# Softcap attention followed by a bilinear feed-forward: a list schedule fixes the order of all five queues

## The chip, the cores and the metric

The kernel runs on one core of one Trainium2 chip. The metric is device time in microseconds (us) of one execution; each version is run several times and the median is compared.

## The reference

```
scale = 1.0 / np.sqrt(q.shape[-1])                     # q, k, v: (4, 12, 448, 64) float32
scores = scale * np.matmul(q, k.transpose(0, 1, 3, 2))
scores = cap * np.tanh(scores / cap)                   # cap = 30
scores = scores - np.max(scores, axis=-1, keepdims=True)
attn = np.exp(scores)
attn = attn / (np.sum(attn, axis=-1, keepdims=True) + 1e-09)
attn_out = np.matmul(attn, v)
x = attn_out.transpose(0, 2, 1, 3).reshape(1792, 768)
out = (x @ w_a) * (x @ w_b) @ w_out                    # w_a, w_b: (768, 1536); w_out: (1536, 768), float64
```

## The kernel before

Attention works on 24 **pairs** (two heads of one batch side by side on the 128 partitions); the feed-forward (FFN) on two **groups** of 896 tokens, and a group needs the output of 12 pairs. This gives three stages: the attention of pairs 0 to 11; the attention of pairs 12 to 23 with the FFN of group 0 put between; the FFN of group 1 alone.

A pair goes through these steps. `load_pair` fetches k and q in eight pieces and v in one, on SP's queue. `prep_pair` turns k and q on DVE (line 213); from pair 12 on each is also split into a rounded high part and the rest (lines 217, 218), and products are made of three parts. `scores` does four chunks of keys, three of 128 for each head and a last one that takes 64 of either: PE writes the chunk into PSUM (line 239, from pair 12 on lines 244 and 247), ACT makes the tanh (line 248) and, for two chunks at once, the exp (line 249), and DVE adds the chunks up for the denominators (lines 253, 256, 257). `attend` multiplies by v (line 269; the last chunk on line 271, a matmul on 64 rows for each head). `normalize` sums over the partitions with matmuls against a selecting matrix (line 282, eight of 112 columns), takes the reciprocal on DVE (line 290), stores it to DRAM as `rd` (line 291) and reads it back spread over 64 partitions for each head as `den` (line 295). `scale` multiplies (line 301), and `split_x` makes the two parts that the FFN reads (lines 310, 311); for the second group they go through DRAM as `xd` and `xl`.

In the FFN a slice of 128 hidden units makes four `ph` products of 18 matmuls with 448 columns (lines 403 to 405), which ACT and DVE empty (lines 408 to 412); after three slices come 14 `po` products of nine matmuls with 384 columns (lines 434 to 436, emptied on lines 438 and 440). Weights come as 64-bit floats: `load64` fetches a tile, `ready_w` converts it in six steps (two on ACT, lines 361 and 362, three on DVE, one on POOL, line 366) and stores it as `wd` for the second group, `split_w` splits it (lines 385, 386).

PSUM holds two score buffers of two banks (`ps_sc`) and four single banks (`ps_1`) for everything else. The order of each queue is the framework's: the loop at the end of the function calls the steps in the order of a string, `run_ffn` advances the FFN generator, and the framework's scheduler then places the instructions by its own estimates, save those marked `keep_in_program_order`.

Of the kernel before, what the change touches and what calls it, by code (L numbers as in the profile page):

```python
# [9 lines left out]
F32 = mybir.dt.float32  # L10
# [107 lines left out]
def kernel(  # L118
# [16 lines left out]
    CP = 112  # L135
    NCH = S // CP
# [13 lines left out]
    PFB = 2  # L150
    Q = 32
    AHEAD = 4
    STRETCH = 1.25

# [4 lines left out]
    rd = [dr.tile([2 * NCH, CP], F32, tag=f"rd{i}", name=f"rd{i}") for i in range(NPAIR)]  # L159
    xd = [dr.tile([P, S], F32, tag=f"xd{i}", name=f"xd{i}") for i in range(NPG)]  # L160
    top = ctx.enter_context(tc.tile_pool(name="top", bufs=1))
    ident = top.tile([P, P], F32, tag="ident", name="ident")
# [7 lines left out]
    pp = fast.enter_context(tc.tile_pool(name="pp", bufs=PFB))  # L170
# [3 lines left out]
    ps_sc = fast.enter_context(tc.tile_pool(name="ps_sc", bufs=2, space=bass.MemoryType.PSUM))  # L174
    ps_1 = fast.enter_context(tc.tile_pool(name="ps_1", bufs=4, space=bass.MemoryType.PSUM))
# [4 lines left out]
    sel = const.tile([P, 2, Q], F32, tag="sel", name="sel")  # L180
# [4 lines left out]

    kz = [const.tile([P, P], F32R, tag=f"kz{x}", name=f"kz{x}") for x in "hl"]


# [4 lines left out]
    def load_pair(pi):  # L193
        b, hp = divmod(pi, NP)
        for nm, src in (("k", k), ("q", q)):
            t = ld.tile([P, S // BLK, BLK], F32, tag=f"ld{nm}", name=f"ld{nm}_{pi}")
            for j in range(2):
                for h in range(D // BLK):
                    rows = slice(j * D + h * BLK, j * D + (h + 1) * BLK)
                    cols = src[b, 2 * hp + j, :, h * BLK : (h + 1) * BLK]  # L200
                    eng = nc.scalar if nm == "q" and pi == 0 else nc.sync
                    eng.dma_start(t[rows], cols.rearrange("(c p) d -> p c d", p=BLK))
            raw[nm, pi] = t
        t = ld.tile([P, 2 * NC3 + 1, D], F32, tag="ldv", name=f"ldv_{pi}", bufs=3)
        nc.sync.dma_start(t, v[b, 2 * hp : 2 * hp + 2].rearrange("j s d -> (j s) d").rearrange("(c p) d -> p c d", p=P))
        raw["v", pi] = t

    def prep_pair(pi):
        stk[pi] = []
        for nm in "kq":  # L210
            t = raw.pop((nm, pi))
            tt = qk.tile([P, S], F32, tag=f"t{nm}", name=f"t{nm}_{pi}")
            nc.vector.transpose(tt, t.rearrange("p c d -> p (c d)"))
            if pi >= NPG:
                hi = qk.tile([P, S], F32R, tag=f"h{nm}", name=f"h{nm}_{pi}", bufs=1)
                lo = qk.tile([P, S], F32R, tag=f"t{nm}", name=f"l{nm}_{pi}")
                nc.scalar.copy(hi, tt)
                nc.vector.tensor_sub(lo, tt, f32(hi))
                tt = (hi, lo)
            stk[pi].append(tt)  # L220
        if pi >= NPG:
            for z, x in zip(kz, stk[pi][0]):
                for j, o in enumerate(own):
                    nc.gpsimd.tensor_copy(z[o, j * R : (j + 1) * R], x[o, krem[j] : krem[j] + R])
# [3 lines left out]
    def scores(pi, hf):  # L228
        tk, tq = stk[pi]
        pf = pp.tile([P, 4 - hf, S], F32, tag=f"pf{hf}", name=f"pf_{pi}_{hf}")  # L230
        for i in range(2):
            c = 2 * hf + i
            n = 2 if c < NC3 else 1
            psc = ps_sc.tile([P, 2, 512], F32, tag="pssc", name=f"psc_{pi}_{c}")
            if pi < NPG:
                for j, o in enumerate(own):
                    at = j * R + c * P if n == 2 else krem[j]
                    to = psc[:, j, :S] if n == 2 else psc[o, 0, :S]
                    nc.tensor.matmul(to, tk[o, at : at + (P if n == 2 else R)], tq[o], start=True, stop=True)  # L239
# [312 lines left out]
```

## Time and profile before

| | |
|---|---|
| median of 3 runs | 762.07 us (759.05 to 763.45) |
| profiled execution | 757.11 us, of which the span from the first to the last instruction 755.2 |
| mean granted clock of TensorE (PE) in it | 0.987 of full speed |
| PE busy | 715.5 us, 95% of the span |
| DVE, ACT, POOL busy | 450.7, 337.4, 141.0 us |

The profile is of one execution. "Busy" is time in which an engine worked on an instruction; a wait is put down to the semaphore that came last. A row of the timeline gives the start, the time, the instruction, and in brackets the idle time before it and what ended it; matmuls overlap, so the time that one costs is read from one start to the next. A float32 matmul shows as two rows.

### The profile page before, as it was taken

What the parts mean: (1) busy time and instruction counts of PE and PEld (TensorE: products, weight loads), DVE (VectorE), ACT (ScalarE), POOL (GpSimd) and SP (SyncE); (2) the same over time, 40 slices, a digit from 0 to 9 for tenths busy, and PEclk for the clock granted to TensorE, in tenths of its full rate; (3) what the DMA queues carried; (4) which work ended last, traced back from release to release, by engine and by line L of the source; (5) the groups of instructions that cost most, each with busy time, mean ns of one, the idle gap of its engine ahead of it and who ended that gap; (6) DMA issues with size and microseconds to landing.
All of it is one profiled execution on the core that took longest, in us unless ns stands there. A gap on an engine that the chain in (4) does not pass through costs nothing.

```text
span 755.2 us, 10285 instructions
## 1 busy us (share of the span) xinstructions
PE 715.5 (95%) x3948; PEld 571.1 (76%) x3948; DVE 450.7 (60%) x648; ACT 337.4 (45%) x426; POOL 141.0 (19%) x160
## 2 busy tenths in 40 slices
PE   5978978999999998999989999999999999999996
PEld 1322225687778777778768789999999999999996
DVE  4687999877856687686785755733124334344322
ACT  5776888665675574375544531021322102102200
POOL 0000135335505444065340310000000000000000
PEclk9999998999999999999999999999999999999999
DMA  7585697675746666254540334632022102201012
GB/s 131 111 170 113 143 226 181 149 232 186 209 107 184 198 180 171 54 159 163 180 162 25 116 119 138 202 104 80 27 62 63 63 22 73 74 22 43 1 42 109
DMA packets 136951, 90.49 MB, mean 120 GB/s; under 512 B 114624, under 2 KB 122560, under 8 KB 136896
## 3 DMA queue, kind: packets, MB, share of 16 engines
q1 hardware_dynamic: 125856, 48.64, 26.4%
q0 software_dynamic: 9184, 40.90, 16.5%
q8 instruction: 33, 0.54, 0.3%
q10 hardware_dynamic: 1856, 0.23, 0.2%
q14 instruction: 22, 0.18, 0.1%
HBM read 67.24 MB, written 22.50 MB: 119 GB/s over the span
## 4 chain that ended last, share of the span: by engine, by line
PE 55%; DMA 17%; DVE 12%; ACT 6%; issue 5%; SPq 2%; POOL 2%; ACTq 0%; DVEq 0%; POOLq 0%
PE po L434 6%; PE po L436 6%; PE po L435 6%; PE pha L405 5%; PE pha L404 5%; PE pha L403 5%; PE phb L405 5%; PE phb L404 5%; PE phb L403 5%; DMA rd<-rec 4%; DMA w64a<-in_moe_w_a_dram 3%; DMA den<-rd 3%; DMA w64o<-in_moe_w_out_dram 3%; PE pv L269 2%; DMA ldk<-in_k_dram 2%
## 5 line engine op out<-in xcount | busy, mean ns | idle before, releaser
L434 PE MATMUL po<-who,gh 128*128 128x384 f32 x336 | 114.5, 341 | 3.5 <-DVE acc L440 2.0
L435 PE MATMUL po<-wlo,gh 128*128 128x384 f32 x336 | 113.7, 338 | 0.0
L436 PE MATMUL po<-who,gl 128*128 128x384 f32 x336 | 113.3, 338 | 0.4 <-DVE gl L412 0.4
L403 PE MATMUL pha<-xhi,wha 128*128 128x448 f32 x288 | 106.1, 368 | 0.0
L404 PE MATMUL pha<-xlo,wha 128*128 128x448 f32 x288 | 105.6, 367 | 0.0
L405 PE MATMUL pha<-xhi,wla 128*128 128x448 f32 x288 | 105.2, 365 | 0.0
L404 PE MATMUL phb<-xlo,whb 128*128 128x448 f32 x288 | 104.9, 364 | 0.0
L403 PE MATMUL phb<-xhi,whb 128*128 128x448 f32 x288 | 104.8, 364 | 0.0
L405 PE MATMUL phb<-xhi,wlb 128*128 128x448 f32 x288 | 104.5, 363 | 0.0
L248 ACT ACTIVATE pf<-psc,capt 128x896 f32<-128x896 f32 x96 | 84.1, 909 | 26.8 <-PE psc L244 12.2
L249 ACT ACTIVATE pf<-pf,capt 128x1792 f32<-128x1792 f32 (+1 forms) x48 | 77.1, 1606 | 1.0
L440 DVE TENSOR_TENSOR acc<-po,acc 128x384 f32<-128x384 f32 x84 | 45.7, 551 | 41.4 <-PE po L436 41.0
L434 PEld LDWEIGHTS po<-who,gh 128*128 128x128 f32 x336 | 63.6, 189 | 7.3 <-DVE acc L440 3.0
L269 PE MATMUL pv<-pf,ldv 128*64 128x448 f32 x288 | 63.3, 554 | 1.6 <-ACT pf L249 1.2
L435 PEld LDWEIGHTS po<-wlo,gh 128*128 128x128 f32 x336 | 63.6, 189 | 1.6 <-issue 1.4
L436 PEld LDWEIGHTS po<-who,gl 128*128 128x128 f32 x336 | 63.5, 189 | 1.6 <-DVE gl L412 1.0
L239 PE MATMUL psc<-tq,tk 64*128 64x448 f32 (+1 forms) x192 | 50.0, 629 | 15.0 <-ACT pf L248 8.0
L410 DVE TENSOR_TENSOR asb<-phb,asb 128x448 f32<-128x448 f32 x48 | 29.7, 619 | 56.8 <-PE phb L405 56.8
L411 ACT CAST gh<-asb 128x448 fp32r<-128x448 f32 x48 | 27.1, 564 | 75.5 <-DVE asb L410 75.2
L403 PEld LDWEIGHTS pha<-xhi,wha 128*128 128x128 f32 x288 | 54.5, 189 | 6.9 <-issue 2.4
L404 PEld LDWEIGHTS pha<-xlo,wha 128*128 128x128 f32 x288 | 54.5, 189 | 5.2 <-issue 1.1
L403 PEld LDWEIGHTS phb<-xhi,whb 128*128 128x128 f32 x288 | 54.0, 188 | 5.2 <-issue 1.3
(99 smaller groups left out, 1040.8 us busy)
## 6 DMA issues: line engine op xcount, KB each, us to landing
w64o<-in_moe_w_out_dram POOLq DMA_DIRECT2D x12, 768.0 KB, 5.8
w64a<-in_moe_w_a_dram POOLq DMA_DIRECT2D x11, 768.0 KB, 6.3
w64b<-in_moe_w_b_dram POOLq DMA_DIRECT2D x11, 768.0 KB, 6.4
ldk<-in_k_dram SPq DMA_DIRECT2D x96, 56.0 KB
ldv<-in_v_dram SPq DMA_DIRECT2D x24, 224.0 KB
den<-rd SPq DMA_DIRECT2D x48, 112.0 KB
ldq<-in_q_dram SPq DMA_DIRECT2D x92, 56.0 KB
out_dram<-acc SPq DMA_DIRECT2D x13, 384.0 KB
```

Source lines behind the costliest of these rows:

```text
L239: nc.tensor.matmul(to, tk[o, at : at + (P if n == 2 else R)], tq[o], start=True, stop=True)
L248: nc.scalar.activation(pf[:, 2 * i : 2 * i + n], psc[:, :n, :S], AF.Tanh, scale=capt[:, 1:2])
L249: nc.scalar.activation(pf, pf, AF.Exp, scale=capt[:, 0:1])
L269: nc.tensor.matmul(t[j * D : (j + 1) * D, :S], tv[:, j * (NC3 + 1) + c], p, start=(c == 0), stop=False)
L403: nc.tensor.matmul(t[:, :S], wh[:, kk], xhi[:, kk, cs], start=(kk == 0), stop=False)
L404: nc.tensor.matmul(t[:, :S], wh[:, kk], xlo[:, kk, cs], start=False, stop=False)
L405: nc.tensor.matmul(t[:, :S], wl[:, kk], xhi[:, kk, cs], start=False, stop=(kk == NK - 1))
L410: nc.vector.tensor_mul(asb[h], t[:, :S], asb[h])
L434: nc.tensor.matmul(t[:, :HALF], gh[:, cs], wh, start=(f == fs[0]), stop=False)
L435: nc.tensor.matmul(t[:, :HALF], gh[:, cs], wl, start=False, stop=False)
L436: nc.tensor.matmul(t[:, :HALF], gl[:, cs], wh, start=False, stop=(f == fs[-1]))
L440: nc.vector.tensor_add(acc[:, ti, hs], t[:, :HALF], acc[:, ti, hs])
```

## The change

All steps become small functions, and each call of one is a job with an engine, a time, a lag and a list of jobs that it needs. The order of PE's jobs is written out (`chain`); every job gets a latest time from the jobs after it, and a list scheduler in the kernel (the last loop below) plays the five engines forward and takes on each the ready job that is due first. The instructions are then issued in that order inside `manual_schedule`, in which the framework moves nothing.

With it come these changes. All four chunks of a pair's scores stand together in the first stage, and two and two in the second. `attend` uses a matmul on 128 rows for the last chunk too, against a copy of v that is zero in the other head's rows. The sums have 14 matmuls of 64 columns in place of eight of 112, and are written into the free columns of the bank of `pv`. PSUM has three score buffers and two `pv` banks in the first stage; in the second two score buffers, one `pv` bank and three FFN banks (the first six FFN products have two). v is loaded in four pieces, for pairs 2 to 11 on POOL's queue; weights after the sixth are fetched, and all `wd` stored, on SP's queue and not POOL's. Weight tiles are taken in the order in which slices need them. The copies for the last chunk (`last_keys`) move from POOL to ACT. Three matmuls on zeros (`warm`) stand ahead of the first scores, and the identity matrix is no longer made on the usual path.

```diff
-    ps_sc = fast.enter_context(tc.tile_pool(name="ps_sc", bufs=2, space=bass.MemoryType.PSUM))
-    ps_1 = fast.enter_context(tc.tile_pool(name="ps_1", bufs=4, space=bass.MemoryType.PSUM))
+    room = {"pv": psum_pool("pv_one", 2), "sc": psum_pool("sc_one", 3)}
...
+        eng = nc.gpsimd if 2 <= pi < NPG else nc.sync
+        if n < 2:
+            part = slice(n * (NC3 + 1), n * (NC3 + 1) + NC3)
+            eng.dma_start(t[:, part.start + n : part.stop + n], src[:, part])
+        else:
+            eng.dma_start(t[own[n - 2], NC3 + n - 2], src[own[n - 2], NC3])
...
-        for c in range(NC3):
-            for j in range(2):
-                p = prob[pi, c // 2][:, 2 * (c % 2) + j]
-                nc.tensor.matmul(t[j * D : (j + 1) * D, :S], tv[:, j * (NC3 + 1) + c], p, start=(c == 0), stop=False)
-        for o in own:
-            nc.tensor.matmul(t[o, :S], tv[o, NC3], prob[pi, 1][o, 2], start=False, stop=True)
...
+        for c in range(2 * hf, 2 * hf + 2):
             for j, o in enumerate(own):
+                p = prob[pi, hf][:, 2 * (c % 2) + (j if c < NC3 else 0)]
+                nc.tensor.matmul(t[o, :S], tv[:, j * (NC3 + 1) + (c if j == 0 else (c + 1) % (NC3 + 1))], p, start=(c == 0), stop=(c == NC3))
...
+                to = t[i * Q : (i + 1) * Q, S : S + SC]
+                nc.tensor.matmul(to, sel[:, m], psum[pi % 2][:, j, c * SC : (c + 1) * SC], start=(m == 0), stop=last)
...
+        if n == 0:
+            room["sc"] = psum_pool("sc_two", 2, "sc_one")
+            room["ff", 0] = psum_pool("ff_a", 2)
+        elif n == FB0:
+            room["pv"] = psum_pool("pv_two", 1, "pv_one")
+            room["ff", 1] = psum_pool("ff_b", 1)
...
+    for pi in range(NPG):
+        for c in range(SUB):
+            scores_of(pi, c)
+        if pi:
+            attend_of(pi - 1)
...
+    ffn(3.6)
+    for pi in range(NPG, NPAIR + 1):
+        attend_of(pi - 1)
+        if pi < NPAIR:
+            for c in range(2):
+                scores_of(pi, c)
+            ffn(GAP / 2)
+            for c in range(2, SUB):
+                scores_of(pi, c)
+            ffn(GAP / 2)
...
+        t, e, xs_ = best
+        x = min((x for x in xs_ if max(x.ready, port if x.shared else 0.0) <= t), key=lambda x: x.due - (SOON if x.fn in (gate, keep_a, collect) else 0.0))
+        (line if e == "PE" else wait[e]).remove(x)
+        x.start, x.end = t, t + x.us + x.lag
+        free[e] = t + x.us
...
+    with tc.manual_schedule(engines={ET.PE, ET.Activation, ET.DVE, ET.Pool, ET.SP}):
+        warm_up()
+        for x in order:
+            x.fn(*x.args)
```

The order of PE's matmuls for one pair in the middle of the first stage, before (psc are scores, pv the products with v, sum the denominators):

```order
L282 MATMUL sum_564<-psum_163,sel 32x112 x8
L269 MATMUL pv_596<-pf_0_538,ldv_425 64x448 x4
L239 MATMUL psc_0_606<-tq_527,tk_525 128x448 x2
L239 MATMUL psc_1_610<-tq_527,tk_525 128x448 x2
L269 MATMUL pv_596<-pf_1_579,ldv_425 64x448 x2
L271 MATMUL pv_596<-pf_1_579,ldv_425 64x448 x2
L239 MATMUL psc_2_647<-tq_527,tk_525 128x448 x2
L282 MATMUL sum_631<-psum_164,sel 32x112 x8
L239 MATMUL psc_3_651<-tq_527,tk_525 64x448 x2
```

and with the change:

```order
L309 MATMUL pv_536<-psum_163,sel 32x64 x14
L255 MATMUL psc_0_583<-tq_476,tk_473 128x448 x2
L255 MATMUL psc_1_592<-tq_476,tk_473 128x448 x2
L255 MATMUL psc_2_602<-tq_476,tk_473 128x448 x2
L255 MATMUL psc_3_607<-tq_476,tk_473 64x448 x2
L297 MATMUL pv_616<-pf_0_516,vb_170 64x448 x4
L297 MATMUL pv_616<-pf_1_534,vb_170 64x448 x4
L309 MATMUL pv_616<-psum_162,sel 32x64 x14
```

The scores, the products with v and the sums of a pair are now one block each, where each of them was cut in two or three before.

DVE's order from one pair's reciprocal (rec) to that pair's multiplication (den), in the same stage, before:

```order
L290 RECIPROCAL rec_506<-sum_497 128x112
L310 CAST xhi<-den_442 128x448
L256 SCALAR_TENSOR_TENSOR psum_163<-pf_1_512,capt,psum_163 64x448 x2
L311 TENSOR_TENSOR xlo<-den_442,xhi 128x448
L257 TENSOR_TENSOR psum_163<-psum_163,pf_1_512 128x896
L253 TENSOR_TENSOR psum_164<-pf_0_538 128x896
L301 TENSOR_TENSOR den_509<-pv_462,den_509 128x448
```

and with the change:

```order
L313 RECIPROCAL rec_587<-pv_536 112x64
L329 TENSOR_TENSOR den_545<-pv_454,den_545 128x448
L288 SCALAR_TENSOR_TENSOR psum_162<-pf_1_534,capt,psum_162 64x448 x2
L345 CAST xhi<-den_545 128x448
L346 TENSOR_TENSOR xlo<-den_545,xhi 128x448
L283 TENSOR_TENSOR psum_162<-psum_162,pf_1_534 128x896
L226 STREAM_TRANSPOSE tk_626<-ldk_509 128x448
L226 STREAM_TRANSPOSE tq_633<-ldq_524 128x448
L386 SCALAR_TENSOR_TENSOR wta_399<-w64a_275,wta_399 128x768
L281 TENSOR_TENSOR psum_163<-pf_0_596 128x896
L313 RECIPROCAL rec_665<-pv_616 112x64
L329 TENSOR_TENSOR den_624<-pv_536,den_624 128x448
```

The multiplication by `den` now stands behind the next pair's reciprocal: more of DVE's work lies between the two.

PE's order where the second stage begins, before, around the sums of a pair (pha and phb are FFN products):

```order
L282 MATMUL pv_1236<-psum_163,sel 32x112
L404 MATMUL pha_0_1_1215<-xlo,wha_0_1034 128x448
L405 MATMUL pha_0_1_1215<-xhi,wla_0_1035 128x448
L282 MATMUL pv_1236<-psum_163,sel 32x112 x7
L404 MATMUL phb_0_1_1309<-xlo,whb_0_1038 128x448
```

and with the change:

```order
L447 MATMUL pha_0_0_1126<-xhi,wla_0_748 128x448
L297 MATMUL pv_1166<-pf_0_1059,vb_171 64x448 x4
L297 MATMUL pv_1166<-pf_1_1076,vb_171 64x448 x4
L309 MATMUL pv_1166<-psum_163,sel 32x64 x14
L260 MATMUL psc_0_1209<-hq_1150,hk_1145 128x448 x2
```

A product of the FFN is no longer cut by attention's matmuls. From the first FFN matmul to the last sums, PE goes from one kind of matmul (scores, products with v, sums, FFN) to another 127 times before and 86 times now.

## Rows read from the trace of the kernel before

**Rows 1.** Windows by stage: us, busy of PE, PEld, DVE, ACT, POOL; clock, DMA share, GB/s.

```profile
0.00:124.00 124.00, 100.79 (x598) 33.11 (x598) 95.95 (x149) 95.34 (x93) 16.01 (x22) 0.96 0.72 153
124.00:455.00 331.00, 320.64 (x1804) 255.90 (x1800) 241.28 (x320) 187.82 (x245) 124.99 (x138) 0.99 0.52 152
455.00:749.00 294.00, 293.96 (x1553) 282.10 (x1551) 112.96 (x179) 54.20 (x89) 0.00 (x0) 1.00 0.22 71
```

**Rows 2.** Timeline of PE, one pair of the first stage without a wait.

```profile
78.36 1.77 PE L239 MATMUL psc<-tq,tk 64*128 64x448 f32 x8
80.06 0.97 PE L269 MATMUL pv<-pf,ldv 128*64 128x448 f32 x4
...
81.86 1.02 PE L239 MATMUL psc<-tq,tk 64*128 64x448 f32 x4
82.81 0.59 PE L282 MATMUL sum<-psum,sel 128*32 128x112 f32 x16
83.33 0.97 PE L239 MATMUL psc<-tq,tk 64*64 64x448 f32 x4
84.23 1.72 PE L269 MATMUL pv<-pf,ldv 128*64 128x448 f32 x8
85.89 1.77 PE L239 MATMUL psc<-tq,tk 64*128 64x448 f32 x8
```

**Rows 3.** Waits of PE, 0 to 128 us: total, times, longest.

```profile
PE psc L239 <- ACT pf L248: 8.0, 3, 4.2
PE psc L239 <- DVE tq L213: 7.0, 1, 7.0
PE sum L282 <- DVE psum L257: 6.4, 6, 2.5
```

**Rows 4.** Timelines of ACT and PE where the first weight tile arrives.

```profile
40.82 0.89 ACT L362 ACTIVATE wta<-w64a 128x768 f32<-128x768 f32 x1 [5.82 <-DMA w64a<-in_moe_w_a_dram]
...
42.66 3.19 PE L239 MATMUL psc<-tq,tk 64*128 64x448 f32 x8 [4.18 <-ACT pf L248]
```

**Rows 5.** Tile sum, 18 to 20 us: duration ns min/median/max, first and last start.

```profile
L282 PE MATMUL sum<-psum,sel x16: 258/260/284, 18.7 to 19.0; 128*32 128x112 f32 x16
```

**Rows 6.** Timeline of PE, the products with v of a pair of the second stage.

```profile
167.92 2.48 PE L269 MATMUL pv<-pf,ldv 128*64 128x448 f32 x12
170.32 0.97 PE L271 MATMUL pv<-pf,ldv 64*64 64x448 f32 x4
171.22 0.59 PE L282 MATMUL pv<-psum,sel 128*32 128x112 f32 x16
```

**Rows 7.** Timeline of PE, from FFN to scores in the second stage.

```profile
147.86 0.47 PE L244 MATMUL psc<-hq,hk 64*128 64x448 f32 x2
148.17 0.36 PE L244 MATMUL psc<-lq,hk 64*128 64x448 f32 x2
148.37 0.37 PE L244 MATMUL psc<-hq,lk 64*128 64x448 f32 x2
```

**Rows 8.** Chain that ended last: start, us, the denominators' transfers, short and long.

```profile
23.82 2.27 DMA rd<-rec
...
94.76 5.44 DMA rd<-rec
...
207.11 7.34 DMA den<-rd
...
234.57 2.79 DMA den<-rd
```

**Rows 9.** Waits of DVE, 0 to 128 us.

```profile
DVE den L301 <- DMA den<-rd: 9.1, 6, 2.7
```

**Rows 10.** Timeline of ACT, the same pair as in rows 2.

```profile
79.43 1.91 ACT L248 ACTIVATE pf<-psc,capt 128x896 f32<-128x896 f32 x2 [0.53 <-PE psc L239]
...
86.34 0.91 ACT L361 ACTIVATE w64a<-w64a 128x768 int32<-128x768 uint32 x1
```

**Rows 11.** Window of the first stage with the highest DMA share, columns as in rows 1.

```profile
100.00:120.00 20.00, 15.31 (x96) 5.21 (x92) 18.25 (x27) 18.47 (x21) 8.12 (x11) 0.91 0.91 225
```

More of the change, by code (lines that the diff above doesn't have):

```diff
@@ L274, in normalize @@
[L274 to L296 removed]
+            nc.vector.tensor_add(t, t, pf[:, 0:2])
@@ new lines, with ffn @@
+    used = {}
+    WARM, SOON = 3, 4.0
+    GAP = 19.4
+    for pi in range(NPAIR):
+        loads(pi, 0.0 if pi < 2 else 5.0)
+        turns(pi)
+        softmax(pi)
+    for pi in range(NPG):
+        for c in range(SUB):
+            scores_of(pi, c)
+        if pi:
+            attend_of(pi - 1)
+    todo, owed = pieces(0), 0.0
+    def ffn(us):
+        nonlocal owed
+        owed += us
+        while todo and owed > 0:
+            owed -= 3.6 if todo[0][0] == "hidden" else 1.56
+            ffn_piece(todo.pop(0))
@@ L454, with limits @@
             nc.vector.memset(f32(z), 0.0)
[L455 to L456 removed]
+        for m in range(SUB):
+            nc.vector.memset(sel[:, m, m * QS : (m + 1) * QS], 1.0)
+    def limits():
         nc.vector.tensor_scalar_mul(capt[:, 4:5], capt[:, 3:4], -1.0)
@@ L514 @@
-        run_ffn(1e18)
+    job("limits", "DVE", 1.3, limits, (), [("turn", "q", 0)])
+    jobs["tanh", 0, 0].needs.append("limits")
+    clock = 7.0
+    kind = None
+    for key in chain:
+        now = "ffn" if key[0] in ("hidden", "project") or (key[0] == "scores" and key[1:] >= (NPG, 3) and key[2] == 3) else key[0]
+        if now != kind:
+            jobs[key].us += 0.15
+        kind = now
+        jobs[key].due = clock
+        clock += jobs[key].us
+    real = list({id(x): x for x in jobs.values()}.values())
@@ new lines, with due @@
+    for x in real:
+        x.from_ = {id(jobs[k]): jobs[k] for k in x.needs if k in jobs}.values()
+        for y in x.from_:
+            y.then.append(x)
+    seen = set()
+    sys.setrecursionlimit(20000)
+    def due(x):
+        if id(x) not in seen:
+            seen.add(id(x))
+            for y in x.then:
+                x.due = min(x.due, due(y) - x.us - (0.0 if y.order_only and y.eng == x.eng else x.lag))
+        return x.due
+    for x in real:
+        due(x)
+    free = dict.fromkeys(LAG, 0.0)
@@ new lines @@
+    line = [jobs[k] for k in chain]
+    wait = {e: [] for e in LAG}
+    for x in real:
+        x.left = len(x.from_)
+        x.ready = x.after
+        if not x.left and x.eng != "PE":
+            wait[x.eng].append(x)
+    order, port = [], 0.0
+    for x in real:
+        x.shared = x.eng == "DVE" and x.fn not in (turn, recip, scale, collect) and not (x.fn is gate and x.args[3] == 0)
+    while len(order) < len(real):
+        best = None
+        for e, xs_ in wait.items():
+            if e == "PE":
+                xs_ = line[:1] if line and not line[0].left else []
+            if xs_:
+                t = max(free[e], min(max(x.ready, port if x.shared else 0.0) for x in xs_))
+                if best is None or t < best[0]:
+                    best = (t, e, xs_)
+        t, e, xs_ = best
[3 more added lines that the diff above has]
+        free[e] = t + x.us
+        if x.fn is conv and e == "POOL":
+            port = t + x.us
+        order.append(x)
+        for y in x.then:
+            y.left -= 1
+            y.ready = max(y.ready, t + x.us if y.order_only and y.eng == x.eng else x.end)
+            if not y.left and y.eng != "PE":
+                wait[y.eng].append(y)
```

651 lines of the change are left out of this document (388 added, 263 removed).

## The prediction

> **What bounds the kernel now.** I read the windows by stage first, then PE's timeline in each stage, then the waits, and last the chain that ended last. PE is what bounds: from 455 us on it is busy for 293.96 of 294 us, and from 124 to 455 for 320.64 of 331 [rows 1]. So the last stage can't move, the middle one has 10.4 us of idle PE, and the first has 23.2 (124 less 100.79). Of these 23.2 the first 7.0 are the wait for q of pair 0 [rows 3], which the change leaves, for its loads start the same way. [...] In sum the first stage loses 21 us to waits and what follows them.
>
> What the waits are is seen in two places. Twice PE's scores wait for a score buffer because ACT stands still: at 35.0 us ACT came to a weight tile that had not landed, idled 5.82 us before it, with a ready tanh behind it in its queue, and PE lost 4.18 us and then ran a block of scores in 3.19 us [rows 4] that takes 1.70 elsewhere [rows 2]. And the sums wait for DVE, 6.4 us in six waits [rows 3], while DVE itself waits 9.1 us for `den` to come back from DRAM [rows 9]. Both are one thing: a queue in order, with an instruction at its head whose data comes later than the scheduler thought. Where nothing is late, a pair takes PE 7.53 us (78.36 to 85.89) [rows 2].
>
> **The change, part by part.** All prices are on the scale of the profiled execution, 757.11 us, of which 755.2 is the span.
>
> *Scores together.* Before, two chunks cost 1.70 us, the third alone 0.95, the last 0.90 [rows 2], 3.55 for a pair. In one block the third follows its like, and the step from one chunk (0.95) to two (1.70) is 0.75, so 1.70 + 0.75 + 0.90 = 3.35. Gain 0.20 for a pair.
>
> *v on 128 rows.* Before, the first two chunks cost 1.66 (84.23 to 85.89) and the last two 1.80 in two shapes (80.06 to 81.86) [rows 2], 3.46. In one shape and one block: 12 rows in 2.40 us [rows 6] make 16 in 3.20 at most, and 3.16 by 1.66 + 2 x 0.75. Gain 0.30 in the first stage. In the second stage it was 2.40 + 0.90 = 3.30 [rows 6], gain 0.14.
>
> *Sums.* No row shows 64 columns. The columns stay the same in total (8 x 112 = 14 x 64 = 896), so the lower end is the 0.52 us of now (82.81 to 83.33) [rows 2]; by the number of instructions, 28 rows for 16, it is 0.91. A fixed start of some 0.15 belongs to either, and the 16 start within 0.3 us, 0.02 apart, while one lasts 0.26 [rows 5]: they overlap four deep, and at 0.02 each 28 take 0.56 to 0.6. I take 0.75, nearer the count than the columns; loss 0.23. [...]
>
> A pair of the first stage then costs PE 3.35 + 3.16 + 0.75 = 7.26 in place of 7.53: 12 x 0.27 = **3.2 us** gained. In the second, attention's products and sums cost 0.09 more a pair: **1.1 us** lost.
>
> *Fewer cuts.* Going from FFN to scores costs 0.31 where the next step costs 0.20 [rows 7], so 0.11 for a change of kind. The order shows 86 such changes for 127: 41 x 0.11 = **4.5 us** gained.
>
> *Waits of the first stage.* The third score buffer lets PE write a chunk further ahead. Two weight tiles are asked for early, on POOL's queue behind v of pair 2, and ACT's first step on them stands behind pair 1's exps, two pairs of some 7 us after the first tanh, so the stop of rows 4 comes only if a tile lands later than about 22 us. On DVE the multiplication by `den` now has the next reciprocal, five more instructions and a weight step ahead of it. Against that stand two things. Scores of two pairs are asked for at the start before any exp is through, so PE has to wait for ACT, whose two tanh take 1.91 [rows 10]; I put 2.5 us of start-up on it. And PE's 7.26 us a pair leaves ACT little: its pair takes up to 6.91 us (79.43 to 86.34) [rows 10], and eight weight steps of 0.9 stand among the 12 pairs, 0.6 a pair, which is more than 7.26 together. Lower end 3 us of waits, upper end the 21 of now. I take 10, because the late transfers remain late (below) but fewer queues stop for them: **11 us** gained.
>
> *Waits of the second stage.* 10.4 us idle and 1% of 331 us in clock, some 3, are there [rows 1]. The order puts some 54 FFN matmuls between two steps of attention, which at 294 us for 1553 [rows 1] is 10 us, and in that time ACT and DVE can finish what the next step needs. I take 6 of the 13 as left (ends 0 and 13): **7 us** gained. One `pv` bank is enough if the round of the denominators is done within a period, which is 331 us for 12 pairs [rows 1], over 25; three FFN banks where there were four suffice as long as an eviction is done while two products run, the shorter of which have nine matmuls, 1.7 us by the same division. Weights on SP's queue come behind that queue's waits; the cover is four converted tiles.
>
> *At no cost.* The zero matmuls run while the first loads are on their way, in the 7.0 us. `last_keys` on ACT adds 0.8 us for each of 12 pairs to an engine that is busy 187.82 of 331 us in that stage [rows 1]; if its queue ran late, scores of the last chunk would be late with it. Reloading x runs behind 14 products of the FFN.
>
> **The sum:** 757.1 - 3.2 + 1.1 - 4.5 - 11 - 7 = **732.5**. The three runs of before lie 1.9 to 6.3 us above the profiled one and their median 5.0; I leave that out and say **732 us**, since a kernel with fewer stops has less to scatter. With the low ends (waits 3 and 0, sums at 0.52, which is 5.5 less over 24 pairs) it is 714; with the high ends (21 and 13, sums at 0.91) 754.
>
> **Rivals.**
>
> *Another resource holds the first stage (chance 0.17).* ACT has no slack there by the count above. DMA has little: its share is 0.72 over 124 us [rows 1], 89 us of work for 16 engines, and the highest 20 us show 0.91, with PE idle for 4.7 of them [rows 11]. The stage that I forecast ends at 110 (124 less 14), a share of 0.81. If the transfers can't be packed over 0.77, it ends at 116; if ACT idles for two weight tiles more, 12 us are lost. Either way 738 to 745, say 741. For it: rows 4 and 11. Against: the same share of 0.72 to 0.91 came with blocks of two or three transfers that all wait for one landing, which an earlier start spreads. [...]
>
> *The round of the denominators decides, and the kernel is slower (0.08).* Place: DVE's multiplication by `den` in the first stage, which waits in order with the adds for the sums and the turns for the next scores behind it. By the order, pair n's multiplication follows pair n+1's reciprocal, so two pairs take at least R + W: R the round from reciprocal to landing, W DVE's other work of a pair, some 6 us (95.95 us over 13 pairs is 7.4 [rows 1], less the two steps). Short transfers make R about 6 (2.27 + 2.79 and an issue) and a pair 6: no wait. The longest rows, 5.44 + 7.34 = 12.8 [rows 8], make 9.4 a pair, 2.1 over the 7.26; in ten pairs 21, in place of my 10: 743. Slower than 761 needs R over 16.2 throughout. It could come so, as SP now has four v pieces, weights and stores in the same queue ahead of `rd` and `den`; R = 18 gives 12 a pair and **770 us**.
>
> *Nothing is gained but the cuts (0.07).* The waits stay at 21 and 13 because they come from late transfers, not from order, and the sums cost 0.91: 754, within 0.5% where the runs lie as they did before: no change.
>
> **How the numbers follow.** The forecast has 0.68 (714 to 744, likeliest 732), the first rival 0.17 (741), no change 0.07, slower 0.08. About 0.5% is what a measurement of this kernel can tell from no change. Faster: 0.68 + 0.17 = 0.85; same 0.07; slower 0.08. The range of 8 in 10 leaves out the slower rival, most of "nothing gained", and the best end: 715 to 751.
>
> **What would show it.** Right: in the profile after, the window up to the first FFN product loses at most 10 us of PE beside the first 7; blocks of 8 rows of scores for two chunks are followed by more of their kind at 0.75; the pair's period is near 7.3; 28 rows of sums take 0.6 to 0.85; the second stage's PE is idle for less than 6 us; the last 294 us are as they were. Wrong: if `den` is what DVE waits for in most pairs; if ACT waits for weight tiles; if FFN products wait for their bank (then three banks are too few); or if the stage of FFN alone grows.

## The result, and the profile after

The changed kernel takes 740.05 us (median of 4 runs, 738.76 to 744.35) against 760.96 us (759.05 to 763.45) on the same chip: a ratio of 0.973, 95% interval 0.968 to 0.979. That is 21 us faster where 29 were forecast; 740 lies inside the range of 715 to 751. The profiled execution took 739.0 us, its span is 737.1. On the scale of profiled executions, on which the forecast was added up, it is 18.1 us faster where 24.6 were forecast.

The windows by stage of the changed kernel (us, busy of PE, PEld, DVE, ACT, POOL; clock, DMA share, GB/s), cut where about the work of [rows 1] is done:

```profile
0.00:116.20 116.20, 99.12 (x714) 40.40 (x716) 85.19 (x144) 88.81 (x92) 38.79 (x52) 0.94 0.78 149
116.20:441.00 324.80, 323.04 (x2012) 266.57 (x2012) 244.41 (x340) 208.26 (x298) 68.36 (x34) 1.00 0.58 162
441.00:731.20 290.20, 289.10 (x1524) 271.76 (x1522) 108.50 (x173) 50.63 (x84) 0.00 (x0) 1.00 0.22 70
```

The first stage gave 7.8 us (124.0 to 116.2) where 14.2 were forecast. PE still stands for 17.1 of its 116.2 us, and for another 4.5 us it works on the zeros of `warm`. The first FFN product starts at 109.71 us where it started at 123.99, but the last pair's v products and the next pair's scores, which stood ahead of it, now stand behind it. All the rest gave 10.3 (757.1 - 124.0 to 739.0 - 116.2), as forecast (4.5 + 7 - 1.1 = 10.4), yet by errors that cancel, as will be seen. PE's idle time in the second stage fell from 10.4 us to 1.8, with the clock at 1.00.

PE's timeline at the start, and one pair without a wait, to lay beside [rows 2]:

```profile
2.75 4.48 PE L710 MATMUL warm<-psum 128*128 128x448 f32 x6 [2.75 <-DVE psum L708]
9.31 5.07 PE L255 MATMUL psc<-tq,tk 64*128 64x448 f32 x16 [2.08 <-DVE capt L718]
18.05 6.20 PE L255 MATMUL psc<-tq,tk 64*128 64x448 f32 x16 [3.68 <-DVE tq L226]
24.18 3.23 PE L297 MATMUL pv<-pf,vb 128*64 128x448 f32 x16
27.34 0.65 PE L309 MATMUL pv<-psum,sel 128*32 128x64 f32 x28
27.92 3.43 PE L255 MATMUL psc<-tq,tk 64*128 64x448 f32 x16
31.27 3.23 PE L297 MATMUL pv<-pf,vb 128*64 128x448 f32 x16
34.43 0.65 PE L309 MATMUL pv<-psum,sel 128*32 128x64 f32 x28
35.01 1.40 PE L255 MATMUL psc<-tq,tk 64*128 64x448 f32 x6
```

A pair takes 35.01 - 27.92 = 7.09 us: scores 3.35 and v 3.16, both as forecast, and sums 0.58 where I took 0.75. The 0.75 was my estimate, 28 rows at 0.02 and a fixed start of 0.15; what was measured is about what the rows alone come to. The 28 rows start in groups of four or three, 6 to 7 ns from row to row and 35 to 60 from group to group (the sums at 27.34 us in the changed kernel).

The start is worse than before: the first scores begin at 9.31 us, not 6.96, and the second pair's at 18.05. These two blocks take 5.07 and 6.20 us where the block at 27.92 us, at a granted clock of 1.00, takes 3.43, 4.4 us more in sum; the granted clock was 0.66, 0.70 and 0.62 in the three stretches of 5 us from 10 to 25 us. (Before, one block of 16 rows took 5.62.) POOL's queue asks for two weight tiles at 4.0 and 4.8 us; these rows of the DMA issues (KB each, median us from issue to landing) say what they took, while k and q of the first two pairs were on their way:

```profile
w64a<-in_moe_w_a_dram POOLq DMA_DIRECT2D x1, 768.0 KB, 7.3
w64b<-in_moe_w_b_dram POOLq DMA_DIRECT2D x1, 768.0 KB, 9.9
```

The waits of PE up to 116.2 us (total, times, longest), beside [rows 3]:

```profile
PE pv L297 <- DVE den L329: 6.4, 4, 2.4
PE psc L255 <- DVE tq L226: 3.7, 1, 3.7
PE warm L710 <- DVE psum L708: 2.7, 1, 2.7
PE psc L255 <- DVE capt L718: 2.1, 1, 2.1
PE pv L309 <- DVE psum L283: 1.8, 2, 1.0
```

ACT, which cost PE 8.0 us, is gone from the list. The multiplication by `den` is new at its head. DVE itself waits for `den` before six of the ten multiplications that it does up to 116.2 us:

```profile
DVE den L329 <- DMA den<-rd: 10.8, 6, 2.4
```

One round, on PE, DVE and SP's queue:

```profile
59.68 0.65 PE L309 MATMUL pv<-psum,sel 128*32 128x64 f32 x28
62.46 0.55 DVE L313 RECIPROCAL rec<-pv 112x64 f32<-112x64 f32 x1
63.24 0.79 SPq L317 DMA_DIRECT2D rd<-rec  x1
67.24 1.11 SPq L323 DMA_DIRECT2D den<-rd  x2
73.39 0.62 DVE L329 TENSOR_TENSOR den<-pv,den 128x448 f32<-128x448 f32 x1 [2.35 <-DMA den<-rd]
74.07 4.92 PE L297 MATMUL pv<-pf,vb 128*64 128x448 f32 x16 [2.41 <-DVE den L329]
```

From the end of the sums (60.3) to the multiplication 13.1 us go by: 2.2 in DVE's queue, 4.8 until `den` can be asked for, 6.1 until it is there. With two `pv` banks, pair n+2's v products need that bank. Between the sums of pair n and those products PE has scores, v, sums and scores to do: 3.35 + 3.16 + 0.58 + 3.35 = 10.4 us, less 0.6 for the multiplication: a round over 9.8 stops PE, unless PE has been held up elsewhere in that time or has FFN products to do first. The rounds of the twelve pairs take 8.2 to 13.1 us, nine of them 10.9 or more; four of them stopped PE. The longest stop is followed by v products that run in part at half clock (4.92 for 3.23; granted clock 0.50 from 75 to 78 us, 0.66 from 74 to 79).

### The profile page after: what moved, and what is told of

Read it like the earlier page. It is cut to its first block, busy times and chain, and to the rows that moved or that the text cites. A ratio compares the mean times of both kernels' runs of the same rounds, so it can differ in the third digit from the quotient of the medians.

```text
span 737.1 us, 10930 instructions
## 1 busy us (share of the span) xinstructions
PE 711.3 (96%) x4242; PEld 578.7 (79%) x4242; DVE 438.6 (60%) x657; ACT 347.7 (47%) x474; POOL 107.1 (15%) x86
## 4 chain that ended last, share of the span: by engine, by line
PE 83%; DMA 7%; SPq 3%; DVE 3%; ACT 2%; issue 1%; POOL 0%; ACTq 0%; DVEq 0%; POOLq 0%
PE phb L445 8%; PE phb L447 8%; PE phb L446 8%; PE pha L445 8%; PE pha L446 8%; PE pha L447 8%; PE po L478 8%; PE po L480 7%; PE po L479 7%; PE pv L297 7%; PE psc L260 3%; DMA den<-rd 3%; SPq L210 2%; DMA rd<-rec 2%; PE psc L255 2%; PE psc L263 1%
## 5 line engine op out<-in xcount | busy, mean ns | idle before, releaser
L297 PE MATMUL pv<-pf,vb 128*64 128x448 f32 x384 | 79.2, 555 | 6.4 <-DVE den L329 6.4
L452 ACT COPY asb<-pha 128x448 f32<-128x448 f32 x48 | 25.6, 533 | 93.3 <-PE pha L447 91.3
L297 PEld LDWEIGHTS pv<-pf,vb 128*64 128x64 f32 x384 | 25.8, 138 | 53.1 <-issue 39.2
```

The source lines that it names most:

```text
L297: nc.tensor.matmul(t[o, :S], tv[:, j * (NC3 + 1) + (c if j == 0 else (c + 1) % (NC3 + 1))], p, start=(c == 0), stop=(c == NC3))
```

## The experiments

| run | median us | ratio to before (95%) | sums of pair 0 start | first FFN product |
|---|---|---|---|---|
| changed kernel | 740.05 | 0.973 (0.968-0.979) | 27.34 | 109.71 |
| weights late, planned anew | 750.82 | 0.987 (0.982-0.992) | 23.35 | 117.28 |
| weights late, same order | 740.86 | 0.975 (0.969-0.981) | 22.23 | 110.87 |
| den on POOL, v on SP | 739.51 | 0.974 (0.969-0.979) | 26.36 | 104.58 |
| framework's order | 820.14 | 1.079 (1.072-1.085) | 29.89 | 162.47 |
| chunks apart | 762.85 | 1.004 (1.001-1.008) | 27.72 | 124.79 |
| two score buffers | 757.33 | 0.997 (0.994-1.000) | 27.23 | 116.65 |
| all tiles on 128 | 738.77 | 0.972 (0.968-0.977) | 24.28 | 109.67 |
| weights 64 above | 736.11 | 0.970 (0.964-0.976) | 24.80 | 109.59 |
| weights 64 below | 733.72 | 0.967 (0.961-0.974) | 27.04 | 109.02 |
| all three | 732.81 | 0.965 (0.959-0.971) | 26.60 | 106.21 |
| all three, planned for | 728.93 | 0.958 (0.954-0.962) | 18.99 | 103.98 |
| kernel before, shifted | 764.02 | 1.005 (1.001-1.010) | 18.66 | 126.06 |

The last two columns come from the profiled executions. Each ratio is to runs of the kernel before made beside that version; their median lay between 759.6 and 763.0 us, so medians of two rows that are less than some 3 us apart show no difference by themselves.

### Was the late start the loss?

```diff
+        if (pi, n) == (2, 0):
+            nc.gpsimd.tensor_copy(mark, stk["q", 1][:, 0:1])
```

This stands at the head of POOL's queue, ahead of v of pair 2 and the weights. First with the need known to the plan, so that it was planned anew:

> The changed kernel with a one-column copy of the turned q of pair 1 at the head of GpSimd's queue, ahead of the v loads of pair 2 and the two weight tiles, so that these 1.7 MB start only when the first two pairs are in. Theory (the start-up loss is these transfers, issued at 1.3 to 5 us with nothing on the device that holds them back): first scores at about 7 us instead of 9.3, second pair's scores by 14 us instead of 18.0, no half-clock pair of scores: 6 to 9 us faster, about 732 us. Rival A (the start-up is late because of the 14 memsets and the warm-up, or because k and q of two pairs go in another order on the load queue): first scores still at 9 us, gain below 2 us. Rival B (the weights are then late for ScalarE and the loss comes back at the first feed-forward product): start-up gained, but a wait of TensorE for the weights at 110 us, gain below 3 us.

The first scores came at 7.82 us, and the kernel was 11 us slower than the changed one. The new plan had put both turns of pair 2 ahead of the last add for the sums of pair 0, DVE stood before them until their loads came (2.80 and 2.49 us), and PE waited 4.33 us for those sums. Rival B expected stops for the weights; PE's stops were for the sums (9.1 us up to 120 us) and for `den` (13.0). With the changed kernel's order kept:

> As the run with the weights late, but the plan is the changed kernel's own: the order on every queue stays word for word, only the one-column copy that waits for the turned q of pair 1 is put at the head of GpSimd's queue. Theory (the start-up loss is the early transfers; the run before lost its gain because the list schedule, planned anew, put a turn of pair 2 ahead of the sums of pair 0 on VectorE, where it waited for its load): first scores at about 7.8 us, second pair's by 13 us, the sums of pair 0 end by 23 us instead of 27.9, and 5 to 9 us are left at the end: 731 to 735 us. Rival (the fixed order loses whatever the start wins, as VectorE's turns stand where slower loads were expected): TensorE waits for psum and den as in the run before, 745 us or more.

The start went as forecast, but nothing was left of it at the end. PE's timeline and its waits up to 117 us:

```profile
7.72 3.43 PE L258 MATMUL psc<-tq,tk 64*128 64x448 f32 x16 [0.47 <-DVE capt L721]
11.30 1.77 PE L258 MATMUL psc<-tq,tk 64*128 64x448 f32 x8 [0.15 <-DVE tq L229]
...
22.23 0.65 PE L312 MATMUL pv<-psum,sel 128*32 128x64 f32 x28 [3.30 <-DVE psum L286]
...
36.99 4.92 PE L300 MATMUL pv<-pf,vb 128*64 128x448 f32 x16 [2.63 <-DVE den L332]
```

```profile
PE pv L300 <- DVE den L332: 9.9, 6, 2.6
PE pv L312 <- DVE psum L286: 5.6, 4, 3.3
```

5.1 us were won at the sums of pair 0 and the first FFN product came 1.2 us later than in the changed kernel: the waits for `den` grew from 6.4 to 9.9 and those for the sums from 1.8 to 5.6. Two runs with the changed kernel's order, all tiles on 128 and weights 64 above, had the sums of pair 0 3.1 and 2.5 us earlier and reached the FFN at the same 109.6. So the theory fell in the form in which I held it: the early weights do make the start late (in the four runs that hold them back the first scores come at 7.7 to 7.9 us), but in this order the rounds that follow set the end of the stage.

### Is it the round of the denominators?

```diff
-        nc.sync.dma_start(rd[pi], pvs[pi][1][0:NSR:QS])
+        (nc.gpsimd if pi < NPG else nc.sync).dma_start(rd[pi], pvs[pi][1][0:NSR:QS])
```

The same for `den`, and `load_v` on SP throughout:

> The changed kernel with the store of the reciprocals and the two loads of the denominators of the first stage on GpSimd's queue, and the v loads, which stood there, on the load queue of k and q. Theory (a denominators' round is long because its loads stand behind 3 to 8 k and q loads on one queue and share its ring): the round shrinks from 9 to about 7 us, the 6.4 us of TensorE's waits for den go: 3 to 6 us faster, about 735 us. Rival (GpSimd's queue takes 4 to 5 us from issue to landing even for 16 KB, so that two transfers in a row there take longer than on the other queue): the round grows to 11 us or more, TensorE waits for den at every pair: 10 us or more slower.

PE's and DVE's waits up to 112 us:

```profile
PE psc L255 <- DVE capt L718: 5.8, 1, 5.8
PE pv L297 <- DVE den L329: 3.5, 3, 1.5
```

```profile
DVE den L329 <- DMA den<-rd: 4.0, 5, 1.5
```

DVE's wait for `den` fell from 10.8 us (to 116.2) to 4.0 and PE's from 6.4 to 3.5. The round itself hardly shrank, from 10.9 to 10.5 us in the mean of pairs 0 to 9, where the theory had 9 to 7 (that its loads share a ring with those of k and q, no run shows): from the reciprocal on it is 0.7 us shorter, and DVE comes 0.3 us later to the reciprocal. From the sums of pair 0 to the first FFN product it is 78.2 us instead of 82.4. (The first scores came only at 13.26; the weights now stood first in POOL's queue.) The stage ends 5.1 us earlier. The whole kernel shows little of it (2.9 us by the profiled spans, 0.5 by the medians): what is behind the first FFN product took 2.2 us more; where, I did not settle.

### What the order and the third buffer are worth

Three runs undo a part of the change each. The last two are planned anew, and their plan also lets a pair's last tanh wait for the one before it; of their edits only the main lines stand here.

```diff
-    with tc.manual_schedule(engines={ET.PE, ET.Activation, ET.DVE, ET.Pool, ET.SP}):
+    with ExitStack():
```

> The changed kernel without its manual schedule: the framework's own scheduler reorders all five queues, as it did before; buffers, pools, sums and the emission order are the changed kernel's. It sets score chunks and v products of the first stage between each other again. Theory (the fixed order is where most of the gain of the two attention stages comes from): the second stage's idle time is back at 8 to 12 us instead of 1.8, 20 or more changes of kind more, and the first stage is no shorter than 116 us: about 752 us. Rival (the buffers did it: three score buffers, one matmul row for the last chunk, shorter sums): within 4 us of the changed kernel, 740 us.

```diff
         for c in range(SUB):
             scores_of(pi, c)
-        if pi:
-            attend_of(pi - 1)
+            if pi and c % 2:
+                attend_of(pi - 1, c // 2)
...
```

> The changed kernel with the first stage's TensorE order as before: two score chunks, half of the v products of the pair before, two score chunks, the other half, sums; planned by the same list schedule, second stage untouched. Theory (a change of kind costs 0.1 us and no more): 11 x 2 changes more, 2.2 us, and the first v half no longer waits for the denominators in time: 742 to 744 us. Rival (the halves stand at better places for ScalarE, since the scores of the next half are ready when the first exponentials run): TensorE's waits for den and psum fall, 735 to 738 us.

```diff
-    room = {"pv": psum_pool("pv_one", 2), "sc": psum_pool("sc_one", 3)}
+    room = {"pv": psum_pool("pv_one", 2), "sc": psum_pool("sc_one", 2)}
...
-        back = 3 if pi < NPG else 2
+        back = 2
```

> The changed kernel with two score buffers instead of three in the first stage, planned anew for them; nothing else. Theory (with the chunks standing together, the third buffer lets TensorE run on while ScalarE is in an exponential): TensorE's waits for ScalarE rise from under 1 us to 1 us or more a pair, 8 to 14 us slower than the changed kernel: 748 to 754 us. Rival (the denominators' round sets the pace and the waits only move from den to ScalarE): within 3 us of the changed kernel, 738 to 743 us.

All three lost more than either theory said, so none of the theories holds as it was written. With the framework's order PE waits 20.8 us for `den` and 13.5 for ACT, and the first FFN product comes at 162 us. The emission order was made for the plan and not for that scheduler, so the 80 us are the price of taking the fixed order away from these pools, not what it gains over the kernel before.

With the chunks apart the whole gain is gone. PE's timeline there, first about a stop, then from one pair's sums to the next without a wait:

```profile
53.91 0.65 PE L309 MATMUL pv<-psum,sel 128*32 128x64 f32 x28
54.49 1.77 PE L255 MATMUL psc<-tq,tk 64*128 64x448 f32 x8
60.84 2.84 PE L297 MATMUL pv<-pf,vb 128*64 128x448 f32 x8 [4.57 <-DVE den L329]
63.60 2.45 PE L255 MATMUL psc<-tq,tk 64*128 64x448 f32 x8
...
67.64 0.65 PE L309 MATMUL pv<-psum,sel 128*32 128x64 f32 x28
...
75.08 0.65 PE L309 MATMUL pv<-psum,sel 128*32 128x64 f32 x28
```

and its longest waits up to 131.5 us:

```profile
PE pv L297 <- DVE den L329: 13.4, 5, 4.6
```

A pair without a wait takes 7.44 us for 7.09. v products now follow half of the scores, so before PE needs the bank it has 7.44 + 1.70 = 9.1 us to do in place of 10.4: a round over some 8.5 stops it, not over 9.8. The rounds, in the new plan, are longer too (8.5 to 14.4 us, 12.0 in the mean of pairs 0 to 9 for 10.9). The waits double (13.4 for 6.4), and the block behind the longest takes more time (2.84 for 1.72; granted clock 0.91 in the mean from 60 to 80 us). Of the 22.8 us by the medians, 15.1 lie ahead of the first FFN product: 7.0 are the longer waits for `den`, some 4 the two more cuts in eleven pairs. How much of the longer waits is due to the smaller room for a round and how much to the longer rounds was not separated. In the rest, some 9 us by the profiles, the order on PE is untouched and the plan is new: PE is idle for 6.6 us between the first FFN product and the end of attention, for 1.8 in the changed kernel.

With two score buffers, PE stands after each two chunks of scores:

```profile
27.81 1.77 PE L255 MATMUL psc<-tq,tk 64*128 64x448 f32 x8
29.94 1.92 PE L255 MATMUL psc<-tq,tk 64*128 64x448 f32 x8 [0.36 <-ACT pf L272]
```

0.36 in most pairs, 3.9 us in ten stops, less than the 1 us a pair of the theory, and one stop of 4.65 for `den`. The run is 17 us slower by the medians and 13 by the profiles, and 6.9 of these lie ahead of the first FFN product. Behind it both kernels have two score buffers, and the loss there comes with the new plan: PE is idle for 6.8 us up to the end of attention, for 1.8 in the changed kernel. So the third buffer is worth some 7 us, and not 17.

### The unchanged last stage

The 1494 products from the end of attention on take 289.6 us in the changed kernel, FFN alone. A piece of the FFN is 18 products of 448 columns; two rows that lie 18 products apart, in the changed kernel:

```profile
465.78 0.37 PE L445 MATMUL pha<-xhi,wha 128*128 128x448 f32 x1
...
469.50 0.37 PE L445 MATMUL pha<-xhi,wha 128*128 128x448 f32 x1
```

and in the kernel before:

```profile
490.60 0.36 PE L403 MATMUL pha<-xhi,wha 128*128 128x448 f32 x1
...
494.20 0.36 PE L403 MATMUL pha<-xhi,wha 128*128 128x448 f32 x1
```

3.72 for 3.60 us: 206.7 ns a product for 200.0, in the same order and at clock 1.00. In the second stage it is mostly 202.7, as a mean over 18 products (single ones lie between 199 and 207). In the kernel before it is 200.0 there too. What changed is where tiles lie, counted from their sizes in the kernels. `rec` shrank from 448 to 256 bytes, so the weight tiles behind it moved: before they began at 128 modulo 256 and `xhi`, `xlo` at 192; now both begin at 192. Four runs moved tiles and left every queue's order as it was, but for the instructions that fill `sel` in two of them.

```diff
-    top = ctx.enter_context(tc.tile_pool(name="top", bufs=1))
+    top = ctx.enter_context(tc.tile_pool(name="top", bufs=1, side="right"))
```

> The changed kernel with the two small tiles capt and bounded moved to the far end of SBUF, so that every tile behind them starts 64 bytes lower, at a multiple of 128 bytes; the order on every engine is the changed kernel's. Theory (layout): the hidden products run at 202.7 and 206.7 ns in the changed kernel and at 200.0 ns before because the changed kernel's shorter rec tile (256 instead of 448 bytes) put the weight tiles 64 bytes off a multiple of 128; then the spacing goes back to 200 ns in both stages, which is worth about 864 x 2.7 ns + 864 x 6.7 ns = 8 us: about 731 us, and the last stage is near 284 us. Rival A (the weight tile and the moving tile must not start at the same place of 128 bytes, since before they stood at 0 and 64): spacing stays at 203 to 207 ns, 739 us. Rival B (the spacing comes from the fixed order and not from addresses): no change, 739 us.

Spacing stayed at 202.7 and 206.7: rival A. In the kernel before:

```diff
-        rec = sm.tile([P, CP], F32, tag="rec", name=f"rec_{pi}", bufs=1)
+        rec = sm.tile([P, CP + 16], F32, tag="rec", name=f"rec_{pi}", bufs=1)
```

> The kernel before with its rec tile 64 bytes wider, which puts its weight tiles 64 bytes off a multiple of 128 and nothing else; the order on every engine is that of the kernel before. Theory (layout) and rival A of the run before: spacing of the hidden products rises from 200.0 to 202.7 to 206.7 ns, 1728 of them, 5 to 11 us: about 766 to 772 us. Rival B (order): no change, 761 us.

```profile
490.06 0.37 PE L403 MATMUL pha<-xhi,wha 128*128 128x448 f32 x1
...
493.78 0.37 PE L403 MATMUL pha<-xhi,wha 128*128 128x448 f32 x1
```

3.72 here too: sixteen more columns in a tile that no FFN product reads slow the kernel before down, by a ratio of 1.005 (1.001 to 1.010). Rival B, the order, is out. Then the other way, in the changed kernel, with `sel` as one strip to make room:

```diff
-        rec = sm.tile([P, SC], F32, tag="rec", name=f"rec_{pi}", bufs=1)
+        rec = sm.tile([P, SC + 16], F32, tag="rec", name=f"rec_{pi}", bufs=1)
...
```

> The changed kernel with a narrower constant tile for the sums (a 64-column strip with one block of ones, read at four offsets, in place of four blocks of 32 columns) and a rec tile 64 bytes wider, so that xhi and xlo start 64 bytes off a multiple of 128 and the weight tiles on one, as in the kernel before; the order is the changed kernel's. Theory (the hidden products lose 2.7 to 6.7 ns each when weight tile and moving tile start at the same place of 128 bytes; both runs on this so far agree): 200.0 ns everywhere, 8 us faster than the changed kernel: about 731 us, the last stage 284 us. Rival (another tile, den or g, was the cause in the shifted kernel before): spacing stays at 203 to 207 ns, 739 us.

```profile
466.64 0.36 PE L446 MATMUL pha<-xhi,wha 128*128 128x448 f32 x1
...
470.28 0.36 PE L446 MATMUL pha<-xhi,wha 128*128 128x448 f32 x1
```

3.64, or 202.3 ns in the mean, in both stages: neither of the two, and half of the gain. With `SC + 48`:

> As the run with the weights off the moving tile, but with rec 448 bytes wide, as before the change, so that the weight tiles lie 128 bytes past a multiple of 256 and xhi and xlo 192: the offset between them, modulo 256, is the one of the kernel before (64 below), where the run before had 64 above. Theory (the offset between weight tile and moving tile, modulo 256, sets the spacing: 0 gives 202.7 or 206.7, 64 above 202.3, 64 below 200.0): 200.0 ns everywhere, 3.9 us less than the run before and 8 us less than the changed kernel: about 731 to 733 us. Rival (the spacing of the kernel before had another cause beside the offset): 202.3 ns, 736 us.

```profile
468.25 0.36 PE L446 MATMUL pha<-xhi,wha 128*128 128x448 f32 x1
...
471.85 0.36 PE L446 MATMUL pha<-xhi,wha 128*128 128x448 f32 x1
```

200.0 again, and the same 1494 products in 283.6 us: 6.0 us in the stage that I had called unchanged. The whole kernel takes 733.72 us, 6.3 less than the changed one by the medians, of the 8 that the spacing makes.

### All together

The two transfers of the round on POOL, the tiles 64 below, and the weights behind q of pair 1:

> Three edits together: reciprocals and denominators on GpSimd's queue with v on the load queue, the first two weight tiles held until q of pair 1 is turned (the plan does not know of it), and the tiles 64 below. Theory (the pace of the first stage is set by the denominators' round; with that shorter, an earlier start stays): sums of pair 0 end by 23 us, then 7.1 us a pair, the first feed-forward product at about 101 us instead of 109.7, 200 ns spacing: 739 - 9 - 8 = 722 us. Rival (the load queue, with 12 issues a pair, then sets the pace): 7.4 us or more a pair with waits of TensorE for tq, 728 to 732 us.

732.81 us, where the theory had 722. From pair 1 on, the pairs up to 54 us and from 77 us follow each other at 7.09. But the sums of pair 0 waited 7.59 us: the loads that come late, now that the two weight tiles start behind q of pair 1, are those of pair 2, whose turn stands ahead of the adds on DVE; DVE stood before it for 8.51 us, until 22.99. So the plan was told, with the first tile behind q of pair 2 and the second behind q of pair 3:

```diff
-            job(("raw", t), "POOL" if t < 6 else "SP", 0.6, load64, (t,), [("conv", t - 2, 5)], 6.0, 12.0)
+            job(("raw", t), "POOL" if t < 6 else "SP", 0.6, load64, (t,), [("conv", t - 2, 5), *([("turn", "q", t + 2)] if t < 2 else [])], 8.0, 12.0)
...
-                job(("load", nm, pi, n), eng, 0.52, load_k, (pi, nm, n), needs, 2.4, after)
+                job(("load", nm, pi, n), eng, 0.52, load_k, (pi, nm, n), needs, 6.0 if 2 <= pi < NPG else 2.4, after)
```

> As the run with all three edits, but the list schedule is told of the weights and plans for them: the first weight tile waits for the turned q of pair 2 and the second for that of pair 3, each taken at 8 us in the plan, and the q and k loads of the first stage from pair 2 on are taken at 6.0 us from issue to landing in the plan where they were taken at 2.4, so that VectorE's turns stand behind the adds for the sums before them. Theory (the start-up loss is an order on VectorE that was planned with loads faster than they are, and the denominators' round; both are mended): sums of pair 0 begin at about 20 us instead of 26.6, no wait for psum over 1 us there, 7.1 us a pair after it, the first feed-forward product at 99 us instead of 106, 725 us. Rival (the transfers need their time wherever they stand, so the wait only moves to a later pair): the first feed-forward product at 104 us or later, 730 us or more.

```profile
18.99 0.65 PE L311 MATMUL pv<-psum,sel 128*32 128x64 f32 x28
19.89 3.60 PE L257 MATMUL psc<-tq,tk 64*128 64x448 f32 x16 [0.25 <-DVE tk L228]
```

728.93 us, the fastest version, 0.958 of before (0.954 to 0.962); the changed kernel stands at 0.973. The start is as forecast, 8 us earlier than in the changed kernel, and 5.7 of these are left at the first FFN product, at the rival's 104. PE still waits 4.5 us for `den` and 4.0 for the sums in that stage, which takes 8.4 us a pair for the 7.09 without waits, and its rounds are no shorter.

## Why the prediction was right, and where it was not

The sign, the range and the price of a pair were right (7.26 forecast, 7.09 measured; only the sums were off, 0.58 for 0.75). The time was 8 us too low, and the parts show larger errors that cancel; that all behind the first stage came out at 10.3 us for 10.4 is luck. Two of the signs of being wrong that I had named came true: DVE waits for `den` in most pairs, and the stage of FFN alone grew.

- **Waits of the first stage** (21 forecast to fall to 10). Next to nothing of these 11 us was won. The 21 were 16.2 of waits and some 5 for the clock, an estimate that no run shows as a time of its own; what the trace of before shows is a granted clock of 0.50 from 42.2 to 45.5, 66.1 to 69.4 and 110.5 to 113.8 us. Idle PE fell from 23.2 to 17.1, but 4.5 us of the busy time are now the zero matmuls; with them the stage loses 21.6 us, and the mean clock fell from 0.96 to 0.94. What the stage did give is mostly the pairs, which gained 0.44 us each and not 0.27, 5.3 us in twelve. Two steps failed, this and the next. One is "the first 7.0 are the wait for q of pair 0, which the change leaves, for its loads start the same way". They don't: v of pair 2 and two weight tiles on POOL's queue now start at the same time, and the scores begin at 9.31. I had noted those tiles and asked only whether ACT would need them early. Two q issues on SP's queue at 8.0 and 11.2 us, while the weights were landing, took 2.7 and 3.1 us, where the median of that queue's q issues is 0.48. What the zero matmuls are worth was not tried.
- **"Short transfers make R about 6 ... no wait."** From the reciprocal to the multiplication it takes 7.8 to 10.9 us in pairs 0 to 9, 9.5 in the mean. Part of it is SP's queue, part the landing (4.0 and 5.6 us in the chain at 63 us), and [rows 8] already had sums of that size. By the forecast's own R + W for two pairs a stop begins at 2 x 7.26 - 6 = 8.5, so with R rightly sized the forecast would have had one. The place was not DVE's order but PE's next use of the `pv` bank, with its limit of 9.8 from the end of the sums. So the mechanism of the second rival is there, in the size of waits of 6.4 us and the half clock behind one of them, inside a kernel that is faster.
- **The first rival's number came out**: it had 741 us and a first stage that ends at 116, because the transfers can't be packed over a share of 0.77; measured are 740, 116.2 and 0.78. But neither of its conditions holds: ACT waits for no weight tile in that stage, and with the same loads the stage can end earlier at a share that is no higher. The run planned for the weights reaches the first FFN product at 103.98 us and has begun the same 714 products at 111.8, for 115.9 in the changed kernel. Up to its first FFN product, columns as in [rows 1], it has a share of 0.75 and the clock at 1.00:

```profile
0.00:104.00 104.00, 88.49 (x683) 34.60 (x683) 80.91 (x134) 83.63 (x83) 24.45 (x43) 1.00 0.75 141
```

- **"Scores together": 0.20 a pair, and cuts at 0.11.** The price of the scores was right; two more cuts a pair cost 0.35 in the run with the chunks apart. The worth was not in it: undone, the change loses its whole gain, and waits for `den`, not cuts, are the largest part of that ahead of the first FFN product. The third score buffer, for which I had no term of its own, carries some 7 us.
- **Waits of the second stage** (13 forecast to fall to 6). 1.8 us of idle PE and no clock loss are left: some 4 better than forecast. One `pv` bank and three FFN banks were enough, as argued.
- **"The last stage can't move."** It grew: 6.0 us there, and some 2 more (864 x 2.7 ns) in the second stage, by the spacing. No term and no rival had this. The sum behind 116 us looks right all the same, so as much was won there beyond the forecast: 4 by the waits, 2 by the sums (0.17 a pair less than forecast, in twelve pairs); where the other 2 came from was not settled.

## What to carry to other kernels

A block order may be worth more by what it lets the other engines do meanwhile than by the changes of kind that it saves: add up what the engine has to do between releasing a buffer and needing it again, and set it against the measured round from the trace. A planned order is as good as its latencies; a transfer that the plan takes at 2.4 us and that lands after 5.7 (a q load of pair 0 in the changed kernel, for which DVE stood 4.91) blocks a whole queue in order, and a "not before" that exists in the plan alone holds nothing back on the chip: the weights were planned from 12 us on and asked for at 4. Zero matmuls that fill a wait count as busy (4.5 us here); take them out before reading what a wait has become. When a small tile changes its size, look at the product spacing of stages that no edit touches.

## What the runs showed of the hardware that was not expected

- The spacing of 448-column products went with where the weight tile begins against the moving tile, in bytes modulo 256 (means over 18 products): at the same place 202.7 ns in the second and 206.7 in the last stage (changed kernel; 206.7 also with all tiles on 128 and in the kernel before, shifted), 64 above 202.3 (weights 64 above), 64 below 200.0 (kernel before, weights 64 below). Only these offsets were tried. Why the same place gives 202.7 in some stretches and 206.7 in others was not found; in the stage of FFN alone of the changed kernel it is 206.7 throughout but for a few products. The products of 384 columns, whose two tiles begin at the same place in both kernels, kept 173.4 ns (stage of FFN alone, before and after).
- Two weight tiles of 768 KB, asked for at 4.0 and 4.8 us in the changed kernel, took 7.3 and 9.9 us; one asked for at 64.6 us, with no other weight tile on its way, took 5.9. Loads came late beside the first two: DVE stood 4.91 us for q of pair 0 and 6.56 for k of pair 1. In the run with all three edits it stood 8.51 for the loads of pair 2.
- A stop of PE was dearer than it was long in some places: in the changed kernel 2.41 us of wait at 74 us were followed by v products in 4.92 us instead of 3.23 (granted clock 0.66 from 74 to 79 us). In the run with the weights 64 above, after 2.08 us at 38 us they took 3.23 (granted clock 1.00 from 20 to 60 us), and after only 1.92 us at 73 us they took 4.92 (0.91 in the mean from 60 to 80 us). What decides was not found.
